# Attention and routed experts on one core: row maxima read from PSUM, low parts moved to GpSimd

## The chip, the cores and the metric

The kernel runs on one core of a Trainium2 chip. Five engines work at the same time, each through its own list of instructions in a fixed order: TensorE (PE in the profile, its weight loads PEld), VectorE (DVE), ScalarE (ACT), GpSimd (POOL) and SyncE (SP, which here issues most transfers). An instruction that waits holds up all that stand behind it on its engine. TensorE writes its results to PSUM, and VectorE and ScalarE read them there. The metric is the device time of one execution in microseconds.

## The reference

Two stages. Attention works on 2 batches x 8 heads, 768 tokens, 64 values a head; each query and key is assigned to the nearest of 16 centroids, and a query sees only keys of its own cluster:

```python
q_assign = argmax(q_n @ c_n)            # 16 centroids a head, all normalised
k_assign = argmax(k_n @ c_n)
mask = q_assign[:, :, :, None] == k_assign[:, :, None, :]
scores = where(mask, scale * q @ k.T, -1e9)
scores = scores - max(scores, axis=-1)
attn = exp(scores); attn = attn / (sum(attn) + 1e-9)
x = attn @ v                            # heads side by side: (2, 768, 512)
```

Then each token goes to one of 8 experts, chosen by the largest logit or, where a local gate says so, by the token before it; the output is the expert's probability times `relu(x @ w1[e]) @ w2[e]` (512 to 1024 to 512).

## The kernel before, in words

The sixteen heads are worked on in eight pairs `u`. 32-bit numbers go through TensorE as two 16-bit parts: a high part (a rounded copy) and a low part (the scaled value less the high part). For a pair, `stA` makes these parts of k, q and v. ScalarE makes the high parts (L216, L219, L226) and the 32-bit copy of v (`VF`, L228), VectorE the low parts in one instruction each (`lo`, L208), and VectorE copies the high parts of k and q into two more tiles, `K2` and `QM`, whose further columns take the cluster one-hots of `stB`, so that a product of `QM` and `K2` is a masked score. These two copies (L214) are called masked copies here. SyncE turns the tiles round by transposing transfers (K1T, QXT, K2T, QMT).

`stC` finds the row maxima. A head has nine units, each 256 queries by 256 keys: two matmuls (L320) into a PSUM tile `pm`, of which there are two in turn. In six of the nine units ScalarE copies `pm` to a 16-bit tile `ev` (L323), and VectorE later passes over each row of `ev` once (`tree`, L332); in the other three VectorE reduces `pm` itself (L325). `fin` then joins the maxima and writes them into `Q2` (L338 to L341), which SyncE transposes into `Q2T` (L342).

`stD` makes the attention of a head, again in nine units: four matmuls (L361, L362) that need K1T, Q1T, K2T and Q2T, an exponential on ScalarE (L364), and, five units later, the product with v. For units in `PVF` (four a head; all nine in the last head) this takes the 32-bit exponentials and `VF` (L389). For the others GpSimd subtracts the high part (`lo`, L370), and three 16-bit matmuls take the place of each 32-bit one (L391 to L393). `nm1` divides (L402 to L409), `nm2` on GpSimd makes the low part of the result `xt` (L413), which SyncE transposes and writes out (L489 to L492) for the logits.

`stC` runs 16 units ahead of `stD`. A hand-written list of places (`at`) gives every other step its place between units, and a scheduler then fixes the order of each engine's instructions when the kernel is built. The expert stage, after the last head, takes expert by expert: gather, two products, scatter; weights arrive in 512 KB pieces that ScalarE and VectorE split (L862, L864). A first expert is started while attention ends.

Of the kernel before, what the change touches and what calls it, by code (L numbers as in the profile page):

```python
# [7 lines left out]
F16 = mybir.dt.float16  # L8
# [14 lines left out]
KP = 28  # L23
# [11 lines left out]
WAX = 1  # L35
PVF = (1, 3, 5, 7)
NEQ = 2
NEM = 99
UORD = [(0, 0), (0, 1), (2, 0), (0, 2), (1, 0), (2, 1), (1, 1), (1, 2), (2, 2)]
OFFS = ((4, 0), (9, 1), (9, 2), (9, 3), (9, 4))  # L40
EVB = 2
EB = 7
K2E = 'V'
V0 = 1
# [5 lines left out]
NM2 = 'G'  # L50
SPLIT = ('kh', 'qh', 'vh', 'vf', 'kl', 'ql', 'vl')
TRO = 0
# [7 lines left out]
VP = -7.0  # L60
QME = 'V'
CAP_LEAD = (200, 176)
# [4 lines left out]
def tile_kernel(ctx, tc, q, k, v, centroids, w_gate, w_local, w1, w2, out):  # L67
# [131 lines left out]
    def stA(u, part=None):  # L199
        R = rows(part)  # L200
        hs = slice(0, 2) if part is None else slice(part, part + 1)

        def src(i):
            return f3(ld[u][i])[:, R]
        k1, k2, qx, qm, q2, vh, vl = (f3(rg(x, u))[:, R] for x in (K1, K2, QX, QM, Q2, VH, VL))

        def lo(out, x, h, sc):
            V.scalar_tensor_tensor(out=out, in0=x, scalar=sc, in1=h, op0=ALU.mult, op1=ALU.subtract)  # L208

        def cp(eng, out, x, h):  # L210
            if eng == "A":
                A.activation(out=out, in_=x, func=AF.Copy, scale=QS)
            else:
                V.tensor_copy(out, h)  # L214
        return dict(
            kh=lambda: A.activation(out=k1[:, :, 0:D], in_=src(0), func=AF.Copy, scale=QS),  # L216
            kl=lambda: lo(k1[:, :, D:2 * D], src(0), k1[:, :, 0:D], QS),
            kt=lambda: SP.dma_start_transpose(out=rg(K1T, u)[:, R], in_=flat(rg(K1, u)[:, hs])),
            qh=lambda: A.activation(out=qx[:, :, 0:D], in_=src(1), func=AF.Copy, scale=QS),  # L219
            ql=lambda: lo(qx[:, :, D:2 * D], src(1), qx[:, :, 0:D], QS),  # L220
            qt=lambda: SP.dma_start_transpose(out=rg(QXT, u)[:, R], in_=flat(rg(QX, u)[:, hs])),
            k2=lambda: cp(K2E, k2[:, :, 0:D], src(0), k1[:, :, 0:D]),
            qm=lambda: cp(QME, qm[:, :, 0:D], src(1), qx[:, :, 0:D]),
            q2=lambda: V.tensor_copy(q2[:, :, 0:D], qx[:, :, D:2 * D]),
            q1=lambda: [SP.dma_start(out=rg(Q1T, u)[i * D:i * D + D, R], in_=rg(QXT, u)[0:D, R]) for i in range(2)],
            vh=lambda: A.activation(out=vh[:, :, 0:D], in_=src(2), func=AF.Copy, scale=VS),  # L226
            vl=lambda: lo(vl, src(2), vh[:, :, 0:D], VS),
            vf=lambda: A.activation(out=f3(rg(VF, u))[:, R, 0:D], in_=src(2), func=AF.Copy, scale=VS),  # L228
        )

    def stB(u, part=None):
# [70 lines left out]
    def stC(g):  # L302
        u, hh = divmod(g, 2)
        st = {}
        order = UORD
        NEV = NEQ + (g % NEM == NEM - 1)
        NQ = 2 * NEV

        def unit(n):
            qp, kc = order[n]  # L310

            def f():
                if n == 0:
                    st["m"] = smp.tile([128, T], F32, name="m", tag="m", bufs=3)
                    st["mx"] = smp.tile([128, T, 3], F32, name="mx3", tag="mx3", bufs=3)
                    st["ev"] = smp.tile([128, 2 * NEV, 768], BF16, name="ev", tag="ev", bufs=EVB)
                pool, tag = (ps_s, "pst") if g == 0 and n % 2 else (ps_m, TM)
                ps = pool.tile([128, 2, 256], F32, name="pm", tag=tag)
                for i in range(2):
                    PE.matmul(out=ps[:, i], lhsT=rg(QMT, u)[:, hh * T + 2 * qp + i, :],  # L320
                              rhs=rg(K2T, u)[:, hh * T + 2 * kc:hh * T + 2 * kc + 2, :], start=True, stop=True)
                if qp < NEV:
                    A.activation(out=st["ev"][:, 2 * qp:2 * qp + 2, kc * 256:kc * 256 + 256], in_=ps, func=AF.Copy)  # L323
                else:
                    mark["V"] = V.tensor_reduce(out=st["mx"][:, 2 * qp:2 * qp + 2, kc], in_=ps, axis=AX.X, op=ALU.max).ins  # L325
            return f

        def tree(i):
            e = st["ev"]
            for j in ((0, 1), (2, 3), (4, 5), ())[i]:  # L330
                if j < 2 * NEV:
                    mark["V"] = V.tensor_scalar(out=e[:, j], in0=e[:, j], scalar1=1.0, scalar2=None, op0=ALU.mult, op1=ALU.max, accum_out=st["m"][:, j:j + 1]).ins  # L332
# [10 lines left out]
        return [unit(n) for n in range(9)], [lambda i=i: tree(i) for i in range(4)] if NQ else [], fin  # L343

    xt = {}

    def stD(g):
# [634 lines left out]
    if True:  # L982
# [44 lines left out]
        for u in range(NP):  # L1027
            a, bb = stA(u), stB(u)
            for nm in SPLIT:
                h2 = [stA(u, p)[nm] for p in range(2)]  # L1030
                a[nm] = lambda h2=h2: [f() for f in h2]
            c0 = 18 * u - LEAD
            if u == 0:
                at(c0 - 60, head0)
            else:
# [84 lines left out]
        for n in range(-90, last):  # L1120
# [6 lines left out]
            if 0 <= n < 9 * NH:  # L1127
# [3 lines left out]
                ds_[g][0][i]()  # L1131
            for off, what in OFFS:
                m = c - (off if c > 10 else min(off, 8))
                if 0 <= m < 9 * NH and m % 9 == 0:
                    if what < 4:
                        if cs_[m // 9][1]:
                            cs_[m // 9][1][what]()
                    else:
                        ins = cs_.pop(m // 9)[2]().ins
                        if m == 0:  # L1140
                            first[2] = ins
            m = n - PVL
# [121 lines left out]
```

## Time and profile before

| what | value |
|---|---|
| median of three runs | 469.55 us (463.31 to 472.13) |
| the profiled execution | 467.98 us, span 466.2 us |
| PE busy | 398.6 us (85%), PEld 349.1 us (75%) |
| DVE busy | 328.5 us (70%), 840 instructions |
| ACT busy | 269.7 us (58%), 508 instructions |
| POOL busy | 143.2 us (31%), 158 instructions |
| attention, the first to the last division of a head (L402) | starts at 57.7 and 270.9 us |
| mean granted clock of TensorE | 0.951 of 2.4 GHz |

Busy time says how much of the span an engine had work in hand, over stages with different limits; the stretch from 45 to 262 us holds most of attention and no expert but the first one's weights. A row of a group of instructions gives the line, engine, operation, tiles written and read, the shape, the count, then the total busy time and the mean of one in ns, then the idle time before them and what ended it. A row of a timeline gives the start and the length in us.

### The profile page before, as it was taken

How to read it: one execution, taken by the hardware profiler on the slowest of the kernel's cores; microseconds unless marked ns; L12 is line 12 of the kernel's file. 1: busy time of each engine (PE TensorE's matmuls, PEld its weight loads, DVE VectorE, ACT ScalarE, POOL GpSimd, SP SyncE). 2: the span in 40 equal slices, each digit the busy share in tenths (PEclk: the TensorE clock that was granted, in tenths of full speed). 3: DMA queues.
4: the chain of work that ended last, by engine and by line, in shares of the span. 5: the costliest groups of instructions: out<-in, count | busy, mean ns of one | idle time of the engine just before them, and what ended most of it. 6: DMA issues, size and time to landing. Idle time of an engine off the chain costs nothing. (4 is left out here: it accounts for less than half of the span.)

```text
span 466.2 us, 12705 instructions
## 1 busy us (share of the span) xinstructions
PE 398.6 (85%) x5039; PEld 349.1 (75%) x5039; DVE 328.5 (70%) x840; ACT 269.7 (58%) x508; POOL 143.2 (31%) x158
## 2 busy tenths in 40 slices
PE   0259879999888799989989999699998699999991
PEld 0237768888777789878879996697797497997870
DVE  7678985887969779787879158566683667666630
ACT  4268857686676767666886430235562656566430
POOL 3003434354343444434735301513022122201021
PEclk9998987999989999989999999799999799999996
DMA  8889998977936758247760712989698599796501
GB/s 171 137 180 206 287 186 194 206 160 155 187 86 139 140 91 159 53 86 161 182 193 19 142 35 55 289 255 231 172 339 305 169 316 277 255 300 215 190 30 33
DMA packets 125213, 81.45 MB, mean 175 GB/s; under 512 B 94537, under 2 KB 110153, under 8 KB 125152
## 3 DMA queue, kind: packets, MB, share of 16 engines
q1 hardware_dynamic: 122448, 73.47, 66.4%
q0 software_dynamic: 2704, 7.15, 4.9%
q8 instruction: 40, 0.66, 0.6%
q14 instruction: 21, 0.17, 0.1%
HBM read 47.04 MB, written 8.63 MB: 119 GB/s over the span
## 5 line engine op out<-in xcount | busy, mean ns | idle before, releaser
L370 POOL TENSOR_TENSOR lo<-e 128x512 f16<-128x512 f32 x75 | 82.2, 1100 | 135.5 <-ACT e L364 135.3
L864 DVE SCALAR_TENSOR_TENSOR W<-wst,W 128x1024 f16<-128x1024 f32 x64 | 77.9, 1222 | 31.6 <-ACT W L862 30.9
L364 ACT ACTIVATE e<-pst 128x512 f32<-128x512 f32 x144 | 83.3, 598 | 20.9 <-PE pst L362 18.9
L918 PE MATMUL g<-XT,W 128*128 128x200 f16 (+8 forms) x288 | 71.9, 261 | 10.0 <-DVE H L922 6.1
L362 PE MATMUL pst<-Q2T,K2T 128*128 128x256 f16 x288 | 74.4, 286 | 5.0 <-DMA Q2T<-Q 5.0
L361 PE MATMUL pst<-Q1T,K1T 128*128 128x256 f16 x288 | 75.1, 284 | 0.0
L389 PE MATMUL o<-VF,e 128*128 128x65 f32 x552 | 74.1, 273 | 0.0
L320 PE MATMUL pm<-K2T,QMT 128*128 128x256 f16 x288 | 55.4, 287 | 21.2 <-DVE mx L325 13.7
L862 ACT ACTIVATE W<-wst 128x1024 f16<-128x1024 f32 x64 | 66.7, 1051 | 9.9 <-DMA wst<-in_moe_w_dram 9.8
L919 PE MATMUL g<-XT,W 128*128 128x200 f16 (+8 forms) x288 | 71.9, 261 | 0.0
L389 PEld LDWEIGHTS o<-VF,e 128*128 128x128 f32 x552 | 70.7, 197 | 1.1
L920 PE MATMUL g<-XT,W 128*128 128x200 f16 (+8 forms) x288 | 70.1, 261 | 0.0
L323 ACT ACTIVATE ev<-pm 128x512 bf16<-128x512 f32 x96 | 55.7, 594 | 20.2 <-PE pm L320 19.9
L332 DVE TENSOR_SCALAR_CACHE_REDUCE ev<-ev 128x768 bf16<-128x768 bf16 x64 | 58.2, 945 | 7.9 <-ACT ev L323 7.9
L921 ACT ACTIVATE H<-g 128x200 f16<-128x200 f32 (+8 forms) x72 | 24.3, 343 | 63.4 <-PE g L920 53.9
L320 PEld LDWEIGHTS <-QMT 128*128 128x128 f16 x288 | 25.3, 106 | 27.7 <-issue 20.5
L391 PE MATMUL o<-VH,e 128*128 128x65 f16 x300 | 40.3, 197 | 0.0
L922 DVE SCALAR_TENSOR_TENSOR H<-g,H 128x200 f16<-128x200 f32 (+8 forms) x72 | 25.9, 373 | 20.2 <-ACT H L921 16.1
L392 PE MATMUL o<-VL,e 128*128 128x64 f16 x300 | 40.1, 195 | 0.0
L929 POOL DMA_INDIRECT out_dram<-ob,scim x16 | 17.7, 1105 | 72.7 <-ACT ob L927 37.6
L393 PE MATMUL o<-VH,lo 128*128 128x65 f16 x300 | 39.4, 196 | 0.0
L361 PEld LDWEIGHTS <-K1T 128*128 128x128 f16 x288 | 31.1, 108 | 9.4 <-issue 5.7
(301 smaller groups left out, 929.2 us busy)
## 6 DMA issues: line engine op xcount, KB each, us to landing
wst<-in_moe_w_dram SPq DMA_DIRECT2D x64, 512.0 KB
xd<-xt SPq DMA_DIRECT2D x12, 384.0 KB
ld_k<-in_k_dram SPq DMA_DIRECT2D x7, 384.0 KB
ld_q<-in_q_dram SPq DMA_DIRECT2D x7, 384.0 KB
ld_v<-in_v_dram SPq DMA_DIRECT2D x7, 384.0 KB
Q1T<-QXT SPq DMA_DIRECT2D x14, 192.0 KB
ld_k<-in_k_dram SPq DMA_DIRECT2D x2, 192.0 KB
ld_q<-in_q_dram SPq DMA_DIRECT2D x2, 192.0 KB
```

The costliest lines, as they stand in the source:

```text
L320: PE.matmul(out=ps[:, i], lhsT=rg(QMT, u)[:, hh * T + 2 * qp + i, :], rhs=rg(K2T, u)[:, hh * T + 2 * kc:hh * T + 2 * kc + 2, :], start=Tru ...
L332: mark["V"] = V.tensor_scalar(out=e[:, j], in0=e[:, j], scalar1=1.0, scalar2=None, op0=ALU.mult, op1=ALU.max, accum_out=st["m"][:, j:j + 1 ...
L361: PE.matmul(out=ps[:, i], lhsT=rg(K1T, u)[:, j, :], rhs=rg(Q1T, u)[:, hh * T + 2 * qc:hh * T + 2 * qc + 2, :], start=True, stop=False)
L362: PE.matmul(out=ps[:, i], lhsT=rg(K2T, u)[:, j, :], rhs=rg(Q2T, g)[:, 2 * qc:2 * qc + 2, :], start=False, stop=True)
L364: mark["A"] = A.activation(out=e, in_=ps.rearrange("p a b -> p (a b)"), func=AF.Exp, scale=SCL).ins
L370: G.tensor_tensor(out=lo, in0=e, in1=eh, op=ALU.subtract)
L389: PE.matmul(out=o[:, t, 0:65], lhsT=e[:, sl], rhs=vf[:, hh, j, 0:65], start=first, stop=False, skip_group_check=True)
L862: A.activation(out=h[:, cs], in_=s[:, cs], func=AF.Copy, scale=WS)
L864: V.scalar_tensor_tensor(out=l[:, cs], in0=s[:, cs], scalar=WS, in1=h[:, cs], op0=ALU.mult, op1=ALU.subtract)
L918: PE.matmul(out=ps, lhsT=lh, rhs=XT[:, 2 * kk, 0:cap], start=(kk == 0), stop=False)
L919: PE.matmul(out=ps, lhsT=lh, rhs=XT[:, 2 * kk + 1, 0:cap], start=False, stop=False)
L920: PE.matmul(out=ps, lhsT=ll, rhs=XT[:, 2 * kk, 0:cap], start=False, stop=(kk == KD - 1))
```

## The change

From the third pair on (`u > 1`) ScalarE scales k and q in place, GpSimd makes all low parts by a plain subtraction, and the high parts are copies of the scaled values; v's low part is taken from `VF`. The masked copies go to ScalarE, and so do two small operations of `vs2`. All nine units of a head are reduced by VectorE from PSUM; `ev`, `tree` and the ScalarE copies are gone, and `fin` has one place in the order. `PVF` has three units in place of four.

```diff
-PVF = (1, 3, 5, 7)
-OFFS = ((4, 0), (9, 1), (9, 2), (9, 3), (9, 4))
-K2E = 'V'
-QME = 'V'
+PVF = (1, 4, 7)
+FINO = 9
+K2E = 'A'
+QME = 'A'
...
+        def scaled(i):
+            if u > 1:
+                A.activation(out=src(i), in_=src(i), func=AF.Copy, scale=QS)
+        def hi(out, i):
+            A.activation(out=out, in_=src(i), func=AF.Copy, scale=1.0 if u > 1 else QS)
         def lo(out, x, h, sc):
-            V.scalar_tensor_tensor(out=out, in0=x, scalar=sc, in1=h, op0=ALU.mult, op1=ALU.subtract)
+            if u > 1:
+                G.tensor_tensor(out=out, in0=x, in1=h, op=ALU.subtract)
+            else:
+                V.scalar_tensor_tensor(out=out, in0=x, scalar=sc, in1=h, op0=ALU.mult, op1=ALU.subtract)
...
-            V.tensor_scalar(out=tf[96:98], in0=st["vs"][96:98], scalar1=1.0 / S, scalar2=None, op0=ALU.mult)
-            V.tensor_copy(tm[96:98], tf[96:98])
+            A.activation(out=tf[96:98], in_=st["vs"][96:98], func=AF.Copy, scale=1.0 / S)
+            A.activation(out=tm[96:98], in_=tf[96:98], func=AF.Copy)
...
-                if qp < NEV:
-                    A.activation(out=st["ev"][:, 2 * qp:2 * qp + 2, kc * 256:kc * 256 + 256], in_=ps, func=AF.Copy)
-                else:
-                    mark["V"] = V.tensor_reduce(out=st["mx"][:, 2 * qp:2 * qp + 2, kc], in_=ps, axis=AX.X, op=ALU.max).ins
+                mark["V"] = V.tensor_reduce(out=st["mx"][:, 2 * qp:2 * qp + 2, kc], in_=ps, axis=AX.X, op=ALU.max).ins
-        def tree(i):
...
-            if NEV < 3:
-                V.tensor_reduce(out=m[:, 2 * NEV:T], in_=st["mx"][:, 2 * NEV:T], axis=AX.X, op=ALU.max)
+            V.tensor_reduce(out=m, in_=st["mx"], axis=AX.X, op=ALU.max)
...
-                    lo = ep.tile([128, 512], F16, name="lo", tag="lo", bufs=5)
+                    lo = ep.tile([128, 512], F16, name="lo", tag="lo", bufs=6)
...
-                    for i, nm in enumerate(("kh", "kl", "kt", "qh", "ql", "qt")):
-                        at(max(c0 - KP + 1.5 * i, L2P + 0.1 * i + 0.1), a[nm])
+                    for i, nm in enumerate(("k", "q")):
+                        for p in range(2):
+                            for j, w in enumerate("shl"):
+                                x = 4.5 * i + 1.5 * p + 0.5 * j
+                                at(max(c0 - KP + x, L2P + 0.1 * x + 0.1), hv[nm + w][p])
```

What the change makes of the order shows at three places. First VectorE, after the small tile `DV` of one pair is written, in the kernel before (`pm` is a score buffer, `mx` its maxima, `ev` the 16-bit copy, K and QX the tiles with low parts):

```order
L287 SCALAR_TENSOR_TENSOR DV_122<-tm,w_104,tf 2x2x64
L325 TENSOR_REDUCE mx_1941<-pm 128x2
L214 COPY K_107<-K_106 128x12x64
L332 TENSOR_SCALAR ev,m<-ev 128x768 x2
L208 SCALAR_TENSOR_TENSOR K_106<-ld_k,K_106 128x6x64 x2
L325 TENSOR_REDUCE mx_1941<-pm 128x2
L214 COPY QM_109<-QX_108 128x12x64
L505 TENSOR_TENSOR acc_537<-lg,acc_537 128x108
L332 TENSOR_SCALAR ev,m<-ev 128x768 x2
L325 TENSOR_REDUCE mx_1941<-pm 128x2
```

The same place in the changed kernel:

```order
L297 SCALAR_TENSOR_TENSOR DV_122<-tm,w_104,tf 2x2x64
L328 TENSOR_REDUCE mx_1969<-pm 128x2 x2
L398 TENSOR_SCALAR r<-o 128x6
L399 RECIPROCAL r<-r 128x6
L401 TENSOR_TENSOR xf<-o,r 128x384
L328 TENSOR_REDUCE mx_1969<-pm 128x2 x5
L501 TENSOR_TENSOR acc_531<-lg,acc_531 128x108
L334 TENSOR_REDUCE m<-mx_1969 128x6
```

Between the reductions there stood two passes over `ev` and the low parts; now there stand reductions and the small operations of `nm1` and `fin`.

GpSimd, in the middle of attention, had `lo` blocks with one `xt` of each head between them and nothing else. In the changed kernel it has, there:

```order
L214 TENSOR_TENSOR VL_117<-VF_120,VH_114 128x384
L409 TENSOR_TENSOR xt<-xf,xt 128x6x64
L366 TENSOR_TENSOR lo<-e 128x512 x4
L214 TENSOR_TENSOR QX_108<-ld_q,QX_108 128x6x64 x2
L214 TENSOR_TENSOR K_106<-ld_k,K_106 128x6x64
L214 TENSOR_TENSOR VL_117<-VF_120,VH_114 128x384
L214 TENSOR_TENSOR K_106<-ld_k,K_106 128x6x64
L366 TENSOR_TENSOR lo<-e 128x512 x2
L409 TENSOR_TENSOR xt<-xf,xt 128x6x64
```

Six low parts a pair stand among the `lo` blocks now, up to five of them in a row, ahead of the `lo` and `xt` behind them.

SyncE, at the end of the first head of a pair, in the kernel before:

```order
L342 DMA_TRANSPOSE Q2T_139<-Q_111 128x6x128
L489 DMA_TRANSPOSE xT<-xt 128x12x128
L490 DMA xd<-xt 768x1x256
L492 DMA xd_61<-xt 768x1x256
L221 DMA_TRANSPOSE QXT_128<-QX_108 128x12x128
L342 DMA_TRANSPOSE Q2T_140<-Q_110 128x6x128
```

and in the changed kernel:

```order
L185 DMA ld_v<-in_v_dram 128x2x384
L231 DMA_TRANSPOSE QXT_128<-QX_108 128x12x128
L485 DMA_TRANSPOSE xT<-xt 128x12x128
L486 DMA xd<-xt 768x1x256
L488 DMA xd_61<-xt 768x1x256
L338 DMA_TRANSPOSE Q2T_140<-Q_110 128x6x128
```

QXT, which reads a low part of q, has moved ahead of the transfers of `xt`; Q2T stands last in both.

## Rows read from the trace of the kernel before

**Rows 1.** Stretches: busy us of PE, PEld, DVE, ACT, POOL; clock, DMA share, GB/s.

```profile
45.00:262.00 217.00, 196.91 (x2679) 177.39 (x2679) 174.93 (x416) 154.28 (x304) 94.68 (x88) 0.95 0.72 150
262.00:466.20 204.20, 182.10 (x2129) 156.66 (x2126) 118.24 (x297) 91.34 (x155) 41.49 (x39) 0.95 0.68 200
```

**Rows 2.** TensorE's waits from 45 to 262 us: total us, times, longest.

```profile
PE pm L320 <- DVE mx L325: 11.9, 13, 2.5
PE pst L362 <- DMA Q2T<-Q: 5.0, 6, 1.1
PE pm L320 <- ACT ev L323: 2.7, 4, 1.3
```

**Rows 3.** Busy times as in the first group, two stretches at the lower clock.

```profile
65.60:75.80 10.20, 9.27 (x66) 7.31 (x63) 5.18 (x12) 6.89 (x14) 2.90 (x3) 0.50 1.12 243
...
161.10:164.50 3.40, 3.25 (x25) 2.66 (x25) 2.19 (x7) 2.15 (x6) 1.04 (x1) 0.50 0.63 119
```

**Rows 4.** Timeline (start us, us) of VectorE, GpSimd and TensorE around one wait.

```profile
54.14 0.54 DVE L208 SCALAR_TENSOR_TENSOR K<-ld_k,K 128x384 f16<-128x384 f32 x1
...
126.59 2.35 POOL L370 TENSOR_TENSOR lo<-e 128x512 f16<-128x512 f32 x2 [1.81 <-ACT e L364]
126.66 2.69 DVE L208 SCALAR_TENSOR_TENSOR K<-ld_k,K 128x384 f16<-128x384 f32 x2
129.28 0.68 DVE L325 TENSOR_REDUCE mx<-pm 128x2 f32<-128x512 f32 x1
130.01 0.38 PE L320 MATMUL pm<-K2T,QMT 128*128 128x256 f16 x2 [2.07 <-DVE mx L325]
```

**Rows 5.** Groups of instructions by form, from 45 to 262 us.

```profile
L370 POOL TENSOR_TENSOR lo<-e 128x512 f16<-128x512 f32 x72 | 79.0, 1103 | 104.8 <-ACT e L364 104.7
L332 DVE TENSOR_SCALAR_CACHE_REDUCE ev<-ev 128x768 bf16<-128x768 bf16 x56 | 50.9, 945 | 7.9 <-ACT ev L323 7.9
L323 ACT ACTIVATE ev<-pm 128x512 bf16<-128x512 f32 x82 | 47.9, 593 | 14.3 <-PE pm L320 14.0
L325 DVE TENSOR_REDUCE mx<-pm 128x2 f32<-128x512 f32 x42 | 28.8, 686 | 5.1 <-PE pm L320 4.9
L413 POOL TENSOR_TENSOR xt<-xf,xt 128x384 f16<-128x384 f32 x14 | 13.9, 992 | 16.8 <-ACT xt L409 16.8
L208 DVE SCALAR_TENSOR_TENSOR QX<-ld_q,QX 128x384 f16<-128x384 f32 x12 | 10.5, 913 | 0.1
L208 DVE SCALAR_TENSOR_TENSOR VL<-ld_v,VH 128x384 f16<-128x384 f32 x12 | 9.3, 780 | 0.1
L208 DVE SCALAR_TENSOR_TENSOR K<-ld_k,K 128x384 f16<-128x384 f32 x10 | 8.7, 886 | 0.6 <-ACT K L216 0.6
```

**Rows 6.** TensorE's timeline: a 32-bit block, a 16-bit block, and what follows each.

```profile
157.21 1.00 PE L389 MATMUL o<-VF,e 128*128 128x65 f32 x8
158.05 0.30 PE L499 MATMUL lg<-wg,xT 128*128 128x18 f16 x6
...
167.15 0.19 PE L391 MATMUL o<-VH,e 128*128 128x65 f16 x1
...
167.51 0.28 PE L361 MATMUL pst<-Q1T,K1T 128*128 128x256 f16 x1
```

**Rows 7.** Groups of ScalarE by form, whole span.

```profile
L228 ACT ACTIVATE VF<-ld_v 128x384 f32<-128x384 f32 x14 | 7.2, 529 | 1.1 <-PE o L389 0.6 <-DMA ld_v<-in_v_dram 0.3
...
L226 ACT ACTIVATE VH<-ld_v 128x768 f16<-128x768 f32 x1 | 0.8, 834 | 0.0
```

**Rows 8.** TensorE's timeline: three more of its waits for VectorE.

```profile
65.05 0.38 PE L320 MATMUL pm<-K2T,QMT 128*128 128x256 f16 x2 [1.61 <-DVE mx L325]
...
145.07 0.38 PE L320 MATMUL pm<-K2T,QMT 128*128 128x256 f16 x2 [1.86 <-DVE mx L325]
...
161.25 0.58 PE L320 MATMUL pm<-K2T,QMT 128*128 128x256 f16 x2 [2.52 <-DVE mx L325]
```

**Rows 9.** SyncE's waits from 45 to 262 us: total us, times, longest.

```profile
SPq L489 <- POOL lo L370: 15.5, 5, 8.7
```

More of the change, by code (lines that the diff above doesn't have):

```diff
@@ L50 @@
 NM2 = 'G'
-SPLIT = ('kh', 'qh', 'vh', 'vf', 'kl', 'ql', 'vl')
+SPLIT = ('ks', 'kh', 'qs', 'qh', 'vh', 'vf', 'kl', 'ql', 'vl')
 TRO = 0
@@ L205, in stA @@
         k1, k2, qx, qm, q2, vh, vl = (f3(rg(x, u))[:, R] for x in (K1, K2, QX, QM, Q2, VH, VL))
+        def scaled(i):
[3 more added lines that the diff above has]
+            A.activation(out=out, in_=src(i), func=AF.Copy, scale=1.0 if u > 1 else QS)
         def lo(out, x, h, sc):
-            V.scalar_tensor_tensor(out=out, in0=x, scalar=sc, in1=h, op0=ALU.mult, op1=ALU.subtract)
+            if u > 1:
+                G.tensor_tensor(out=out, in0=x, in1=h, op=ALU.subtract)
+            else:
+                V.scalar_tensor_tensor(out=out, in0=x, scalar=sc, in1=h, op0=ALU.mult, op1=ALU.subtract)
         def cp(eng, out, x, h):
             if eng == "A":
-                A.activation(out=out, in_=x, func=AF.Copy, scale=QS)
+                A.activation(out=out, in_=x, func=AF.Copy, scale=1.0 if u > 1 else QS)
             else:
@@ L215, in stA @@
         return dict(
-            kh=lambda: A.activation(out=k1[:, :, 0:D], in_=src(0), func=AF.Copy, scale=QS),
+            ks=lambda: scaled(0),
+            kh=lambda: hi(k1[:, :, 0:D], 0),
             kl=lambda: lo(k1[:, :, D:2 * D], src(0), k1[:, :, 0:D], QS),
             kt=lambda: SP.dma_start_transpose(out=rg(K1T, u)[:, R], in_=flat(rg(K1, u)[:, hs])),
-            qh=lambda: A.activation(out=qx[:, :, 0:D], in_=src(1), func=AF.Copy, scale=QS),
+            qs=lambda: scaled(1),
+            qh=lambda: hi(qx[:, :, 0:D], 1),
             ql=lambda: lo(qx[:, :, D:2 * D], src(1), qx[:, :, 0:D], QS),
@@ L226, in stA @@
             vh=lambda: A.activation(out=vh[:, :, 0:D], in_=src(2), func=AF.Copy, scale=VS),
-            vl=lambda: lo(vl, src(2), vh[:, :, 0:D], VS),
+            vl=lambda: lo(vl, f3(rg(VF, u))[:, R, 0:D] if u > 1 else src(2), vh[:, :, 0:D], VS),
             vf=lambda: A.activation(out=f3(rg(VF, u))[:, R, 0:D], in_=src(2), func=AF.Copy, scale=VS),
@@ L304, in stC @@
         st = {}
-        order = UORD
-        NEV = NEQ + (g % NEM == NEM - 1)
-        NQ = 2 * NEV
         def unit(n):
-            qp, kc = order[n]
+            qp, kc = UORD[n]
             def f():
@@ L342, in fin @@
             return SP.dma_start_transpose(out=rg(Q2T, g), in_=q2.rearrange("p t d -> p (t d)"))
-        return [unit(n) for n in range(9)], [lambda i=i: tree(i) for i in range(4)] if NQ else [], fin
+        return [unit(n) for n in range(9)], fin
     xt = {}
@@ L1028, in tile_kernel @@
             a, bb = stA(u), stB(u)
+            hv = {nm: [stA(u, p)[nm] for p in range(2)] for nm in SPLIT}
             for nm in SPLIT:
-                h2 = [stA(u, p)[nm] for p in range(2)]
-                a[nm] = lambda h2=h2: [f() for f in h2]
+                a[nm] = lambda h2=hv[nm]: [f() for f in h2]
             c0 = 18 * u - LEAD
@@ L1054, in tile_kernel @@
                         at(L2P, load2)
-                    for i, nm in enumerate(("kh", "kl", "kt", "qh", "ql", "qt")):
-                        at(max(c0 - KP + 1.5 * i, L2P + 0.1 * i + 0.1), a[nm])
+                    for i, nm in enumerate(("k", "q")):
[3 more added lines that the diff above has]
+                                at(max(c0 - KP + x, L2P + 0.1 * x + 0.1), hv[nm + w][p])
+                        x = 4.5 * i + 3.5
+                        at(max(c0 - KP + x, L2P + 0.1 * x + 0.1), a[nm + "t"])
                     for i in range(4):
@@ L1069, in tile_kernel @@
                     at(c0 - 3, a["q1"])
-                    at(c0 - 16.2, a["vh"])
-                    at(c0 - 15, a["vl"])
-                    at(c0 - 14.5, a["vf"])
+                    for p in range(2):
+                        at(c0 - 16.2 + 2 * p, hv["vf"][p])
+                        at(c0 - 15.7 + 2 * p, hv["vh"][p])
+                        at(c0 - 15.2 + 2 * p, hv["vl"][p])
                     at(c0 - 7.5, bb["vs"])
@@ L1131, in tile_kernel @@
                 ds_[g][0][i]()
[L1132 to L1141, printed above, removed]
+            m = c - (FINO if c > 10 else 8)
+            if 0 <= m < 9 * NH and m % 9 == 0:
+                ins = cs_.pop(m // 9)[1]().ins
+                if m == 0:
+                    first[2] = ins
             m = n - PVL
```

8 lines of the change are left out of this document (removed).

## The prediction

> **What bounds the kernel now.** I read the busy times by stretch first, then TensorE's waits in the attention stretch, then the granted clock behind those waits, then single timelines around a wait.
>
> The attention stretch, 45 to 262 us, is nearly half of the span [rows 1]. TensorE is busy in 196.91 of its 217.00 us, VectorE in 174.93, ScalarE in 154.28, GpSimd in 94.68. So TensorE sets the pace, VectorE is the next engine at 81%, and GpSimd has more than half its time free. The reader is to see that 20.1 us of TensorE's stretch are idle, and that three waits account for nearly all of them [rows 2]: 11.9 us for a score buffer (`pm`) that VectorE has not yet read, 5.0 us for the transposed Q2T, 2.7 us for a `pm` that ScalarE has not yet copied out. The granted clock is the second loss. In four pieces of the stretch, of 10.2, 3.4, 3.4 and 3.4 us, it is 0.50, the lower level of 1.2 GHz [rows 3], where the first and the third of them stand; each follows one or two waits of TensorE of 0.9 to 2.5 us. Work at half the clock loses at most half of the 20.4 us, 10.2 us.
>
> What makes VectorE late is in [rows 4]. TensorE waits 2.07 us for a `pm`, until 130.01. In that time VectorE runs two low-part instructions on L208, 2.69 us for the two, while GpSimd runs two `lo` subtractions, 2.35 us for the two; only then does VectorE start the reduction at 129.28 that frees the buffer. The same form on L208 takes 0.54 us at 54.14, where GpSimd is not shown with it. The mean of the form in the stretch is 0.78 to 0.91 us [rows 5], so this collision is common and not a single event.
>
> **The change part by part**, in the profiled execution of 467.98 us, which is 1.6 us under the median of the three runs.
>
> Three 32-bit blocks a head instead of four. A 32-bit block takes TensorE from 157.21 to 158.05, 0.84 us; a block of twelve 16-bit matmuls from 167.15 to 167.51, 0.36 us [rows 6]. Fifteen heads change one block (the last head stays all 32-bit): 15 x 0.48 = 7.2 us of TensorE's own time at the full clock. Nothing lies beside it, because TensorE is the pacing engine. **-7.2 us**, bounds 0 (were each saving eaten by a wait) and 7.2.
>
> Row maxima straight from PSUM. The stretch holds 82 ScalarE copies, 47.9 us, and 56 passes over the copied rows on VectorE, 50.9 us [rows 5]. They give way to 82 more reductions of 0.686 us, 56.3 us. On VectorE alone the swap costs 5.4 us. TensorE's wait for ScalarE's copy can't occur any more: **-2.7 us**. But all nine units of a head now wait for VectorE, where three did. The Trainium skill (VectorE: DVE Perf Modes, Rules for kernel authors) speaks against this edit: a reduction is the slowest VectorE operation, to be restructured on a hot path, and a matmul's output may rather be copied to SBUF first. By that rule VectorE gets longer, which the 56.3 against 50.9 bears out; taken alone it would add up to 5.4 us where I book a gain.
>
> Low parts of q, k, v to GpSimd. From the third pair on, 36 instructions leave VectorE. The stretch has 34 on L208, 28.5 us, of which the four of the second pair stay (about 3.4), so some 25 us go [rows 5]. VectorE's balance is 174.9 - 50.9 - 25 + 56.3, at most 155 us, and less by the masked copies and the small operations on `tf` and `tm`, which leave too. GpSimd gets 36 x 0.992 (the form 128x384 of L413) = 35.7 us and 15 x 1.103 = 16.5 us for the fifteen new `lo` blocks: 94.7 becomes 146.9 us, 74% of a stretch of 198 us. ScalarE loses 47.9 and gets 24 in-place scalings x 0.529 = 12.7 us, 14 wide masked copies x 0.834 = 11.7 us [rows 5, 7] and some twenty smaller ones, below 0.53 us each: still under 145 us. The exponentials that TensorE needs sit behind these on ScalarE; I cost that at nothing because ScalarE's idle share grows. If that cover is gone, an exponential starts one copy, 0.83 us, late.
>
> VectorE's wait, now 11.9 us over 13 times. Four waits make 8.06 us of it: 2.07 [rows 4], 1.61, 1.86 and 2.52 [rows 8]. By VectorE's timeline ahead of each, the three of 2.07, 1.86 and 2.52 us, 6.45 together, stand behind L208 or the passes on L332, which leave; the one of 1.61 stands behind L208 and behind a one-hot product and a small line of `fin` that stay. One end is 0. The other end goes with the number of units: the remaining 5.45 us over the 48 units that VectorE reads are 0.114 us a unit, and 144 units would make 16.3 us, more than now. I take 6, nearer to the lower end, since much of the 5.45 us stood behind leaving work too: **-5.9 us**, bounds -11.9 and +4.4.
>
> Clock. Three of the four slow pieces, 3.4 us each, follow waits for VectorE or ScalarE of 1.3 to 2.5 us. If those waits shrink the pieces go: half of 10.2 is **-5.1 us**. The first piece, 65.6 to 75.8, I leave: it has a Q2T wait in it and the DMA share of its stretch is 1.12 [rows 3]. Bounds 0 and 10.2.
>
> What is late next. SyncE issues the transposes in order. The one of `xt` already waits 15.5 us for GpSimd [rows 9], and the Q2T of the odd head stands behind it (the last place shown in the part on the change). With the low parts in front of it on GpSimd, `xt` comes up to three instructions of 0.99 us later, and so do K1T and QXT, which now wait for GpSimd themselves. TensorE's 5.0 us for Q2T therefore stay, and I add **+3.0 us**, one such delay; bounds 0 and one delay in each of the eight pairs, 24 us, of which the free time on SyncE hides most.
>
> Sum: 467.98 - 7.2 - 2.7 - 5.9 - 5.1 + 3.0 = 450.1. The stretches before 45 and after 262 us keep their work; the start's reductions on VectorE (9 x 0.686 = 6.2 us a head) take the place of copies and passes that took it about as long. I predict **450 us** for the median.
>
> **Rivals.**
> - *All of it goes.* VectorE is never late, the clock stays up, Q2T comes in time: 467.98 - 7.2 - 11.9 - 2.7 - 5.0 - 10.2 = 431. For it: the waits' cause leaves. Against: Q2T's chain gets GpSimd ahead of it. 431 to 440 has a chance of 0.13.
> - *The waits only change their names.* The block swap and ScalarE's wait are gained, the rest comes back as short waits: 468 - 9.9 = 458, and up to 463. For it: VectorE stays above 70% and collides more often with a GpSimd that is busy 74% instead of 44% of the stretch, in the instructions that it keeps (one-hot products, the q copy, the DV line). 0.19, two thirds of it below 460.2. The Trainium skill (GPSIMD Engine Reference, 8. Key points) has the rule for it: GpSimd shares its SBUF interfaces with VectorE and contends with VectorE instructions that have two SBUF inputs; the trace agrees (1.35 us each in rows 4, 0.54 alone).
> - *VectorE's wait goes with the units* (slower). If each unit that VectorE reads costs what it does now, 11.9/48 = 0.25 us, then 144 units cost 35.7: 468 + 23.8 - 9.9 = 482. It decides from 21.8 us of such waits, 0.15 us a unit. Against it: 6.45 of the 11.9 us stand behind instructions that leave. 0.05.
> - *GpSimd becomes the bound* (slower). Its 139 instructions in the stretch at a mean of 1.63 us would take 226 us: 477. It decides from a mean of 1.42 us (198 us); now it is 94.68/88 = 1.08, and 1.17 in the collision of rows 4. 0.04. The Trainium skill (GPSIMD Engine Reference, 4.1 Engine selection) says not to put two-input elementwise work on GpSimd, being about twice as slow; the trace agrees (0.99 against 0.54), and this is the rule by which the move would lose.
> - *No effect*: the stretch is not on the path, and what follows waits for something else. TensorE is busy 182.10 of the 204.20 us after it [rows 1], so an earlier end moves everything. 468, 0.06.
>
> **How the numbers follow.** The forecast, 442 to 457, has 0.53. This kernel's runs spread from 463.3 to 472.1, so 2%, 9.4 us, is about what can be told; the line is 460.2. Faster: 0.53 + 0.13 + 0.12 = 0.78. Same: 0.07 + 0.06 = 0.13. Slower: 0.09. The range 437 to 462 leaves out the lower half of the first rival, the slower cases and no effect, about 0.21.
>
> **What would show it.** In the changed profile: 360 matmuls on each of the three 16-bit lines and 432 on the 32-bit one; the mean of the reductions still near 0.69 us; TensorE's `pm` waits at about 6 us for VectorE and none for ScalarE; VectorE's busy time in attention under 155 us, GpSimd's near 147 with a mean near 1.05; fewer pieces at 0.50. The prediction is wrong if `pm` waits stay above 12 us, if Q2T waits grow past 8 us, or if TensorE waits for GpSimd's `lo` or `VL`.

## The result, and the profile after

The changed kernel takes 449.19 us (median of four executions) where the kernel before took 467.87 us beside it on the same chip: a ratio of 0.962, with a 95% interval of 0.951 to 0.973. One of the four took 969.08 us at a granted clock of 1.0, for a reason that no trace shows; the ratio leaves it out, as it does the longest of the kernel before, 472.13 us, and the other three, 447.58 to 449.77 us, have a median of 448.62. The forecast was 450. The profiled execution has 447.58 us and a span of 445.8 us, at a mean granted clock of 0.979 instead of 0.951.

The stretches after, with the columns of [rows 1], and below them the only piece of attention that is left at the lower clock [rows 3]:

```profile
45.00:241.60 196.60, 179.10 (x2686) 161.91 (x2682) 143.51 (x322) 130.28 (x259) 135.98 (x135) 0.99 0.76 155
241.60:445.80 204.20, 182.06 (x2155) 157.24 (x2153) 119.37 (x300) 93.00 (x157) 42.50 (x40) 0.96 0.70 205
48.20:51.60 3.40, 3.06 (x36) 2.22 (x37) 1.25 (x2) 3.04 (x7) 2.62 (x4) 0.50 1.04 289
```

The second row is cut to the length of the second stretch of before, 204.20 us counted back from the end, and holds the same work (TensorE busy 182.06 us, before 182.10): the gain lies ahead of it, as the prediction had it. VectorE fell from 81% to 73% of the attention stretch, GpSimd rose from 44% to 69%. TensorE's waits in attention, to be held against [rows 2]:

```profile
PE pst L357 <- ACT e L360: 5.3, 9, 1.2
PE pm L326 <- DMA QMT<-QM: 4.9, 3, 2.3
PE pm L326 <- DVE mx L328: 2.6, 8, 0.7
PE sim L259 <- DMA K1T<-K: 2.6, 1, 2.6
PE rp L533 <- DVE sc L531: 1.5, 1, 1.5
```

All three waits of before are gone or small: VectorE 11.9 to 2.6 us, ScalarE's copy 2.7 to none, Q2T 5.0 to none. But 14.3 us of new ones (5.3 + 4.9 + 2.6 + 1.5) stand in their place, so TensorE is idle for 17.5 of 196.6 us where it was for 20.1 of 217. The groups that answer to [rows 5]:

```profile
L366 POOL TENSOR_TENSOR lo<-e 128x512 f16<-128x512 f32 x86 | 92.8, 1094 | 43.2 <-ACT e L360 43.1
L328 DVE TENSOR_REDUCE mx<-pm 128x2 f32<-128x512 f32 x123 | 82.1, 685 | 28.2 <-PE pm L326 28.0
L409 POOL TENSOR_TENSOR xt<-xf,xt 128x384 f16<-128x384 f32 x14 | 13.5, 966 | 4.5 <-ACT xt L405 4.5
L214 POOL TENSOR_TENSOR QX<-ld_q,QX 128x384 f16<-128x384 f32 x12 | 10.8, 923 | 3.6 <-DVE r L398 1.5 <-DVE Q L234 1.4 <-ACT QX L210 0.8
```

The reduction costs 685 ns as before (686), the low part on GpSimd 923, and `lo` stayed at 1,094 (1,103) although GpSimd has much more to do. GpSimd still waits 43 us for exponentials, so it isn't the bound.

Where the new waits come from is seen on ScalarE and TensorE around one of them (start us, us):

```profile
98.69 0.94 ACT L210 ACTIVATE K<-ld_k 128x384 f16<-128x384 f32 x2 [2.53 <-DMA K1T<-K]
99.53 0.58 ACT L360 ACTIVATE e<-pst 128x512 f32<-128x512 f32 x1
100.16 0.27 PE L357 MATMUL pst<-Q1T,K1T 128*128 128x256 f16 x1 [1.22 <-ACT e L360]
```

ScalarE stands 2.53 us before a copy of the next pair, because the tile of the high and low parts of k (`K1` in the kernel, `K` in the row) has one buffer and the transposition of the pair before still reads it. The exponential behind it in ScalarE's list comes late, and TensorE waits 1.22 us for it. The masked copies that moved to ScalarE wait in the same way, for the tile `K2`, which the row calls `K` too:

```profile
ACT K L220 <- DMA K2T<-K: 8.1, 5, 3.6
```

### The profile page after: what moved, and what is told of

Its sections match the earlier page's. It is cut to its first block, busy times and chain, and to the rows that moved or that the text cites. A ratio compares the mean times of both kernels' runs of the same rounds, so it can differ in the third digit from the quotient of the medians.

```text
span 445.8 us, 12748 instructions
## 1 busy us (share of the span) xinstructions
PE 384.8 (86%) x5099; PEld 336.4 (75%) x5099; DVE 296.4 (66%) x738; ACT 248.6 (56%) x470; POOL 189.5 (43%) x209
## 5 line engine op out<-in xcount | busy, mean ns | idle before, releaser
L366 POOL TENSOR_TENSOR lo<-e 128x512 f16<-128x512 f32 x90 | 96.9, 1091 | 72.5 <-ACT e L360 72.4
L328 DVE TENSOR_REDUCE mx<-pm 128x2 f32<-128x512 f32 x144 | 95.7, 685 | 30.7 <-PE pm L326 30.4
L358 PE MATMUL pst<-Q2T,K2T 128*128 128x256 f16 x288 | 71.1, 273 | 0.0
L385 PE MATMUL o<-VF,e 128*128 128x65 f32 x432 | 56.7, 270 | 0.0
L385 PEld LDWEIGHTS o<-VF,e 128*128 128x128 f32 x432 | 53.4, 192 | 0.7
L388 PE MATMUL o<-VL,e 128*128 128x64 f16 x360 | 47.1, 192 | 0.0
L387 PE MATMUL o<-VH,e 128*128 128x65 f16 x360 | 47.0, 194 | 0.0
L389 PE MATMUL o<-VH,lo 128*128 128x65 f16 x360 | 44.0, 193 | 0.4 <-POOL lo L366 0.4
L901 POOL DMA_INDIRECT xg<-xd,gim x16 | 16.8, 1049 | 50.5 <-DMA XT<-xg 38.6
L915 PEld LDWEIGHTS <-W 128*128 128x128 f16 x288 | 28.6, 99 | 9.6 <-issue 7.2
```

Source lines behind the costliest of these rows:

```text
L358: PE.matmul(out=ps[:, i], lhsT=rg(K2T, u)[:, j, :], rhs=rg(Q2T, g)[:, 2 * qc:2 * qc + 2, :], start=False, stop=True)
L385: PE.matmul(out=o[:, t, 0:65], lhsT=e[:, sl], rhs=vf[:, hh, j, 0:65], start=first, stop=False, skip_group_check=True)
L915: PE.matmul(out=ps, lhsT=lh, rhs=XT[:, 2 * kk + 1, 0:cap], start=False, stop=False)
```

## The experiments

For every run I read the same ledger from its profiled execution, in attention from 45 us to the last head's division: TensorE's idle time in waits, the part of it for VectorE's maxima and for Q2T, and what the clock cost (half of the time at 0.50, an upper bound). The last column is read off TensorE's order: how many units of scores stand between a head's last unit of maxima and its own first unit of scores, the mean over heads 3 to 16. `fin` and the transposition Q2T have to fit in there; it is called the lead below.

| run | median us | ratio to before (95%) | last division | idle | VectorE | Q2T | clock | lead |
|---|---|---|---|---|---|---|---|---|
| before | 465 to 468 | | 270.9 | 19.9 | 11.9 | 5.0 | 10.2 | 5.4 |
| changed | 449.19 | 0.962 (0.951 to 0.973) | 252.2 | 16.9 | 2.6 | 0 | 1.7 | 6.9 |
| e1 four blocks | 453.78 | 0.973 (0.967 to 0.978) | 257.4 | 12.9 | 3.0 | 0.4 | 6.8 | 7.5 |
| e2 three blocks alone | 469.22 | 1.004 (1.000 to 1.009) | 269.7 | 26.3 | 9.0 | 8.2 | 8.5 | 4.3 |
| e3 PSUM maxima alone | 454.09 | 0.972 (0.966 to 0.978) | 257.7 | 10.4 | 5.0 | 2.5 | 1.7 | 5.2 |
| e4 low parts alone | 476.14 | 1.023 (1.016 to 1.029) | 277.7 | 25.5 | 4.7 | 13.3 | 6.8 | 2.6 |
| e5 PSUM maxima, three blocks | 454.23 | 0.974 (0.968 to 0.979) | 258.6 | 14.5 | 10.0 | 3.0 | 5.1 | 4.6 |
| e6 as e4, masked copies on VectorE | 476.53 | 1.025 (1.018 to 1.031) | 278.8 | 27.4 | 4.3 | 15.9 | 8.5 | 2.6 |
| e7 changed, two buffers | 447.59 | 0.958 (0.952 to 0.964) | 252.0 | 13.2 | 4.0 | 0.7 | 5.1 | 7.2 |
| e8 changed, masked copies on VectorE | 450.53 | 0.966 (0.961 to 0.971) | 255.6 | 13.2 | 6.5 | 0 | 8.5 | 7.1 |
| e11 changed, low parts on VectorE | 455.94 | 0.978 (0.974 to 0.983) | 254.6 | 18.4 | 6.3 | 5.3 | 1.7 | 5.3 |
| e12 changed, two buffers and two blocks | 467.10 | none (458.26 to 469.50) | 271.3 | 28.8 | 6.7 | 4.7 | 13.7 | 7.9 |

e9 and e10 are told apart below. One row is one execution, and not always one near the median: that of e2, 461.61 us, is the shortest of twelve, that of e11, 451.08, the shortest of six, that of e3, 456.49, the longest of six. With 448.62 in place of 449.19 for the changed kernel each difference from it below is 0.6 us larger; with only three executions behind it, its interval overlaps those of e1 and e5, so differences of 5 us are best estimates.

**e1: the change with four 32-bit blocks a head.**

```diff
-PVF = (1, 4, 7)
+PVF = (1, 3, 5, 7)
```

> The changed kernel with four 32-bit blocks a head again, all else as changed. Theory (TensorE paces attention with its own work): each of 15 blocks costs 0.48 us more, so 449 + 7.2 = 456 us, TensorE's waits from 45 us to the end of attention stay near 17 us. Rival (the block swap is swallowed by waits for GpSimd and ScalarE, whose fifteen lo blocks leave here): within 2 us of 449.

453.78 against 449.19: within the full change the swap is worth 4.6 us of the 7.2. TensorE waits in e1:

```profile
PE pst L357 <- ACT e L360: 4.9, 5, 3.0
PE pm L326 <- DVE mx L328: 3.0, 7, 0.9
```

In attention TensorE is busy 9.3 us longer than in the changed kernel (199.0 against 189.7), of which up to 5.1 belong to the clock (6.8 against 1.7), and idle 4.0 us less. So the swap's work is partly taken back in the changed kernel as waits, the one for QMT above all (4.9 against 1.8 here). Neither forecast is met: the time lies between the two, and the waits fell to 12.9 us.

**e2: three blocks alone, on the kernel before.**

```diff
-PVF = (1, 3, 5, 7)
+PVF = (1, 4, 7)
```

> The kernel before with three 32-bit blocks a head, nothing else changed. Theory: TensorE has 7.2 us less work but VectorE's collisions with GpSimd stay and get fifteen lo instructions more, so less than the full 7.2 us arrives: 462 to 466 against 468. Rival (the swap is worth the same anywhere): 460.5.

469.22, no gain in the median (1.004, 1.000 to 1.009); both forecasts had one. The twelve executions spread from 461.61 to 474.41 us, and even the three shortest, with a mean of 464.0, are only 2.4 us below the mean of the kernel before, a third of the 7.2. TensorE's waits:

```profile
PE pm L320 <- DVE mx L325: 9.0, 9, 1.7
PE pst L362 <- DMA Q2T<-Q: 8.2, 5, 3.1
```

TensorE has the shorter work, and waits instead: its idle time is 26.3 instead of 19.9 us.

**e3: maxima from PSUM alone, on the kernel before** (with the one place of `fin`; low parts, copies and blocks as before).

```diff
-                if qp < NEV:
-                    A.activation(out=st["ev"][...], in_=ps, func=AF.Copy)
-                else:
-                    mark["V"] = V.tensor_reduce(...)
+                mark["V"] = V.tensor_reduce(...)
```

> The kernel before with all row maxima read from PSUM by VectorE, nothing else changed (four blocks, low parts and masked copies still on VectorE). Theory (the relief of VectorE comes from the low parts, the maxima alone lengthen it by about 5 us): TensorE waits more than 11.9 us for VectorE and none for ScalarE; 466 to 474. Rival (the two-step way through ScalarE and back was the late part): waits for VectorE under 6 us, 455 to 460.

454.09, 12.2 us below the kernel before: this part alone brings two thirds of the whole. My theory fails, and what the rival said of the waits holds, at a time just below its range. The edit takes out ScalarE's copies and VectorE's passes together; which of the two is worth the 12.2 us no run separates. Its stretch:

```profile
45.00:248.00 203.00, 191.46 (x2709) 174.36 (x2708) 170.79 (x389) 116.57 (x222) 97.00 (x90) 0.99 0.78 159
```

TensorE's waits in it:

```profile
PE pm L316 <- DVE mx L318: 5.0, 14, 0.5
PE pst L348 <- DMA Q2T<-Q: 2.5, 3, 1.3
```

VectorE is fuller than before (84% of the stretch, before 81%) and yet less late: the longest wait for it is 0.5 us instead of 2.5. The stretch is at clock 0.99.

**e4: the low parts alone, on the kernel before** (scaling in place, plain subtraction on GpSimd, masked copies and two small operations of `vs2` on ScalarE, all at the places that they have in the changed kernel's order).

```diff
-K2E = 'V'
+K2E = 'A'
-QME = 'V'
+QME = 'A'
...
+            if u > 1:
+                G.tensor_tensor(out=out, in0=x, in1=h, op=ALU.subtract)
```

> The changed kernel with the row maxima as before (ScalarE copies, passes on VectorE) and four 32-bit blocks, so that only the low parts on GpSimd, the in-place scaling and the masked copies on ScalarE are left of the change (lo has five buffers as before, for space). Theory (collisions of low parts with GpSimd made VectorE late): TensorE's waits for VectorE fall from 11.9 to under 5 us, 456 to 460. Rival (VectorE's passes over the copies made it late, or ScalarE, at 154 + 25 us of work, becomes late): waits for a pm of 10 us or more, 464 to 470.

476.14, slower by 1.6 to 2.9%, which neither forecast had. Two lines of TensorE and one of VectorE show how:

```profile
PE pst L375 <- DMA Q2T<-Q: 13.3, 10, 3.4
PE pm L333 <- DVE mx L338: 4.7, 8, 0.9
...
DVE ev L345 <- ACT ev L336: 23.1, 13, 5.0
```

The wait that the low parts were blamed for falls from 11.9 to 4.7 us, as the prediction wanted, but the wait for Q2T grows by 8.3. VectorE now stands 23.1 us (before 7.9 [rows 5]) for ScalarE's 16-bit copies, with the masked copies, the scalings and the exponentials on ScalarE as well; and the lead in TensorE's order fell to 2.6 units.

**e5: maxima from PSUM and three blocks.**

```diff
-PVF = (1, 3, 5, 7)
+PVF = (1, 4, 7)
```

(on e3)

> The kernel before with the row maxima read from PSUM and three 32-bit blocks a head; low parts and masked copies stay on VectorE. Theory now (reading PSUM directly is what ends VectorE's lateness, the low parts' move gives nothing of its own): the block swap brings its 4.6 us on top of 454.1, so 448 to 451, as the whole change. Rival (with fifteen more lo blocks the low parts on VectorE collide with GpSimd, as where the block swap alone brought nothing): 454 to 458, and the move of the low parts is worth the difference to 449.

454.23, as e3 and as the rival had it. The swap's gain goes into one wait:

```profile
PE pm L316 <- DVE mx L318: 10.0, 14, 1.8
PE pst L348 <- DMA Q2T<-Q: 3.0, 4, 0.9
```

GpSimd has fifteen more `lo` blocks, and VectorE is busy in 178.59 of the 204 us from 45 us on. During these 14 waits and the 1.5 us ahead of each, VectorE spends 10.2 us on low parts and masked copies; in e3 it spent 3.5 there.

**e6: e4 with the masked copies back on VectorE.**

```diff
-K2E = 'A'
+K2E = 'V'
-QME = 'A'
+QME = 'V'
```

> The version with only the low parts moved (row maxima through ScalarE copies, four blocks, 476 us), with the masked copies of k and q back on VectorE. Theory (ScalarE, which got scalings and masked copies and waits in order for transposes, makes its copies of pm late, these VectorE's passes, these the maxima and Q2T): VectorE's wait for those copies falls from 23.1 us to under 12, TensorE's wait for Q2T from 13.3 to under 8, 466 to 470. Rival (the low parts on GpSimd hold up the transposes on SyncE): Q2T waits stay above 11 us, 474 to 478.

476.53, with 15.9 us for Q2T in 12 waits. That the masked copies on ScalarE made e4 slow is refuted; VectorE's wait for ScalarE's copies fell only to 19.5 us. The rival's numbers came true, but not its reason. VectorE, SyncE and TensorE around the longest of the 12 waits (start us, us):

```profile
82.74 0.16 DVE L354 TENSOR_SCALAR Q<-m 128x12 f16<-128x12 f32 x1
82.93 1.21 SPq L355 DMA_TRANSPOSE Q2T<-Q  x1
87.29 0.37 PE L375 MATMUL pst<-Q2T,K2T 128*128 128x256 f16 x1 [3.23 <-DMA Q2T<-Q]
```

SyncE starts the transposition 0.03 us after the last write of `fin`, and within 0.13 us in all 12, so no low part holds it up there; in e4 it does so in eight of the ten and is 1.4 and 1.5 us late in two. It is `fin` that comes late for TensorE's order. What e4 and e6 share, and no other run has, is the lead of 2.6 units, with the low parts on GpSimd beside maxima that go through `ev`.

**e7: the changed kernel with two buffers for `K2` and `QM`.**

```diff
-    K2 = ring(tokp, "K2", [128, 2, T, 128], F16, 1)
+    K2 = ring(tokp, "K2", [128, 2, T, 128], F16, 2)
-    QM = ring(tokp, "QM", [128, 2, T, 128], F16, 1)
+    QM = ring(tokp, "QM", [128, 2, T, 128], F16, 2)
```

> The changed kernel with two buffers instead of one for the masked tiles K2 and QM, all else as changed. Theory (ScalarE waits up to 3.6 us in its order for the transposes of these tiles, 9.7 us in all, and the exponentials and QMT behind it come late): these waits go, TensorE's waits for exponentials and QMT (10.2 us) halve, 442 to 446. Rival (the waits are slack of ScalarE, the transposes are late for SyncE's own order): 448 to 451.

```profile
PE pm L326 <- DVE mx L328: 4.0, 11, 0.7
...
PE pst L357 <- ACT e L360: 1.6, 4, 0.8
PE pm L326 <- DMA QMT<-QM: 1.0, 1, 1.0
```

The waits named fall as the theory has it, from 5.3 to 1.6 us for exponentials and from 4.9 to 1.0 for QMT. The time is 447.59, between the two forecasts, and its interval overlaps that of the changed kernel: of the 7.6 us won, 3.9 came back as other waits, and up to 3.4 went to the clock (5.1 us instead of 1.7). It is the fastest kernel here by its median, but it isn't shown to be faster than the change. `K1`, whose wait was shown above as the example, kept its one buffer, and ScalarE still waits for it (4.9 us in the change):

```profile
ACT K L210 <- DMA K1T<-K: 6.0, 2, 3.8
```

So, by this run, most of the late exponentials came from the masked tiles and not from `K1`.

**e8: the changed kernel with the masked copies on VectorE.**

```diff
-K2E = 'A'
+K2E = 'V'
-QME = 'A'
+QME = 'V'
```

> The changed kernel with the masked copies of k and q back on VectorE (K2E and QME), all else as changed. Theory (in-order waits on ScalarE delay exponentials): waits of TensorE for exponentials fall from 5.3 us to under 2, waits for VectorE rise from 2.6 us by less than 3: 446 to 450. Rival (VectorE, now in front of every pm, must not wait for transposes): waits for VectorE above 7 us, 452 to 456.

450.53: the place of the masked copies is worth 1 or 2 us, if anything; the intervals overlap. VectorE's wait grows to 6.5 us, by more than the theory allowed and less than the rival wanted; the one for exponentials falls to 2.5.

**e9: the kernel before with more lead, e10: with more lead and three blocks.**

```diff
-LEAD = 16
+LEAD = 20
```

(e10 also with `PVF = (1, 4, 7)`)

> The kernel before with the maxima 20 instead of 16 units ahead of attention; no work is removed. Theory (the first half of attention before is bound by a chain of each head: last maxima, their joining, the transpose Q2T, first score): the Q2T waits of 5.0 us fall below 2 and part of the 11.9 us for VectorE with them, so the time is 458 to 463 us. Rival (VectorE's own amount of work makes the waits): more lead only moves them, Q2T falls but the waits for VectorE stay at 10 us or more, 464 to 469 us.

> The kernel before with 20 units of lead and three 32-bit blocks a head. Theory (three blocks bring their 7.2 us wherever the chain of Q2T has slack): 4 to 7 us below the run with 20 units of lead and four blocks. Rival (the fifteen more 16-bit blocks bring fifteen more subtractions on GpSimd, which lengthen VectorE's low parts and copies, so VectorE takes the gain): within 1.5 us of that run, with waits for VectorE of 9 us or more.

In both the parts of v of a later pair are written, with a lead of 20, into a tile that the last products of an earlier head still have to read (in e9 those of the fourth pair from 56.87 us on, while the second head's last product starts at 71.0), so x is another one and the experts get other tokens. The whole times, 499.22 and 493.50 us (1.071 and 1.057), are therefore not comparable, and only attention is read. In e9 the wait for Q2T falls to 2.0 us, and nothing is won: the last division starts at 279.7, later than before's 270.9, and the waits for VectorE stay:

```profile
PE pm L320 <- DVE mx L325: 10.3, 12, 1.9
...
PE pst L362 <- DMA Q2T<-Q: 2.0, 3, 1.4
```

The theory that the chain through Q2T alone bounds the kernel before falls; the rival's wait is there, though both missed the time. In e10 the order keeps a lead of only 4.8 units and the wait for Q2T is back at 9.8 us. Attention is 7.3 us shorter than in e9 (272.4 against 279.7), near the 7.2 of the swap, and the whole 5.7 us, as the theory had it, although the chain of Q2T has no slack there and VectorE's low parts are where they were. So the swap can pay without the other parts; but e10's attention is still longer than before's, and no version that is faster than before shows this.

**e11: the changed kernel with its low parts on VectorE**, same instruction, other engine.

```diff
-                G.tensor_tensor(out=out, in0=x, in1=h, op=ALU.subtract)
+                V.tensor_tensor(out=out, in0=x, in1=h, op=ALU.subtract)
```

> The changed kernel with the low parts from the third pair on back on VectorE, as the same plain subtraction of in-place scaled values; all else as changed. Theory (with three blocks VectorE is the engine that lacks room, and the move to GpSimd makes it): VectorE goes from 70% to about 82% of attention, waits for VectorE from 2.6 to 7 to 10 us, time 453 to 457 us. Rival (the room on VectorE is not needed, masked copies on ScalarE made it already): 447 to 451 us.

455.94, 6.8 us above the change and as slow as e5, as the theory has it. VectorE's share of the time from 45 us to the last division is 79%, by the same count 70% in the change, and the wait for it is 6.3 us, a little less than forecast; and the lead is down to 5.3 units, with Q2T back:

```profile
PE pm L326 <- DVE mx L328: 6.3, 10, 1.5
PE pst L358 <- DMA Q2T<-Q: 5.3, 5, 3.2
```

**e12: two 32-bit blocks a head, on e7.**

```diff
-PVF = (1, 4, 7)
+PVF = (2, 6)
```

> The changed kernel with two buffers for K2 and QM, and two instead of three 32-bit blocks a head. Theory (TensorE sets the pace, so that each block swapped gives its 0.48 us fifteen times): 7.2 us below the run with two buffers alone (447.6), less up to half of it in new waits, 440 to 444 us. Rival (GpSimd, at 66% of attention, gets fifteen more subtractions of 1.09 us and is late with lo and the low parts): 446 to 452 us, with waits of TensorE for lo, K1T or QXT of over 6 us together.

467.10, with runs from 458.26 to 469.50, so spread that no ratio is given; each of them is slower than any run of e7. Both theories missed it, and the first fails outright: less work for TensorE doesn't go on paying. The waits that the rival named, for `lo`, K1T and QXT, come to 2.5 us instead of over 6. The longer ones, in an execution of 467.77 us (what the one of 458.26 waited for isn't known):

```profile
PE pst L357 <- ACT e L360: 7.7, 5, 2.5
PE pm L326 <- DVE mx L328: 6.7, 13, 1.2
...
ACT e L360 <- PE o L388: 17.8, 21, 5.2
```

ScalarE waits 17.8 us (1.0 in the change) for a product that still reads the buffer of an exponential, and TensorE in turn for exponentials. The lead swings from 7 to 12 units and ends at 3 and 1 in the last two heads. Whether the order or GpSimd's `lo` makes these products late I didn't test.

## Why the prediction was right

The total is right, 450 against 449.19, and so is the place; several of its steps were not, and their errors cancel, so that a microsecond separates the two is luck. In the two profiled executions attention ends 18.7 us earlier (270.9 to 252.2), of 20.4 us in the span. Of the 18.7, TensorE's busy time gives 16.1 (205.8 to 189.7) and its waits 3.0 (19.9 to 16.9), less 0.4 that rounding and small gaps leave. The sum had the swap and the clock at 12.3 and the waits at 5.6. The signs that it named are there: no wait for ScalarE's copy, VectorE busy 143.5 us (forecast under 155), GpSimd 136.0 (near 147).

- *The block swap, -7.2, "nothing lies beside it, because TensorE is the pacing engine"*: the work is gone (16.1 us of busy time less 8.5 of clock leave 7.6), but that it is worth 7.2 is wrong as a rule. It was worth 4.6 in the full change (e1), nothing that can be told on the kernel before (e2) and nothing on PSUM maxima alone (e5), where VectorE's wait grew by 5.0. The lower bound, each saving eaten by a wait, is what two of these three cases come near to. TensorE set the pace only between its waits.
- *ScalarE's copy, -2.7*: right, no such wait is left in the change and in e3.
- *VectorE's wait, -5.9*: 9.3 went. The direction is right, the cause half. The 13 waits of before have, in them and in the 1.5 us ahead of each, 9.1 us of low parts and masked copies on VectorE and 9.0 us of passes over `ev`. Taking either away leaves less than half: 5.0 us without the passes (e3), 4.7 without the low parts and masked copies (e4). I had put the low parts first [rows 4] and booked the maxima as 5.4 us more on VectorE. The rule of the Trainium skill that I weighed there (VectorE: DVE Perf Modes, Rules for kernel authors) would have made this edit a loss; VectorE got fuller in e3, as it says, and the kernel 12.2 us faster, so the measurement decides against it. The page advises the copy to SBUF only for many operations on the output, which I didn't say there; here each copied row got one pass.
- *Clock, -5.1*: 8.5 went (10.2 to 1.7). The first piece, which I left, went as well. The loss doesn't follow the sum of the waits: e3 has 1.7 at 10.4 us idle, the change 1.7 at 16.9, e7 and e8 5.1 and 8.5 at 13.2. Single microseconds of it are not to be forecast from this.
- *Q2T stays at 5.0 and +3.0 is added*: wrong, it went to none. This is the step that failed. I looked at what stands ahead of the transposition on SyncE [rows 9]; but in four of the six waits of before SyncE started it within 0.1 us of the last write of `fin`, so it wasn't SyncE that made those. In the change SyncE does wait for the low parts as foreseen:

```profile
SPq L231 <- POOL VL L214: 12.0, 4, 4.6
```

  It costs nothing: the new order has 6.9 units between a head's last maxima and its first scores instead of 5.4. The transposition that SyncE starts latest, at 125.17, 2.95 us after `fin`, isn't needed until 133.77. Over all runs the wait for Q2T goes with that number: 13.3 and 15.9 us at 2.6 units, 3.0 to 9.8 at 4.3 to 4.8, 2.5 to 5.3 at 5.2 to 5.4, and at most 0.7 from 6.9 on (but for e9 with 2.0, and e12 with its uneven 4.7). In e9, where the lead alone was raised (5.4 to 7.1), the wait fell from 5.0 to 2.0; elsewhere the engines changed with it. That lead is a property of the built order, which a reader could count before running anything; the prediction shows SyncE's order and didn't count TensorE's.
- *Left out of the sum*: 14.3 us of new waits for exponentials, QMT, K1T and one small product. The prediction said of exponentials that they come late if ScalarE's cover is gone and costed it at nothing, because ScalarE's idle share grows. That share did grow (29% to 34% of the stretch), but part of it is now ScalarE standing ahead of an exponential before a copy into a single-buffered tile. e7 shows it for QMT and the masked copies.

The parts don't add up: alone they change the time by -12 (maxima), +10 (low parts) and +3 us (blocks, by the medians; the interval just reaches none), together -17 to -19. With the maxima from PSUM, the low parts' move is worth nothing at four blocks (e1 453.8, e3 454.1) and 5.0 at three (449.2, e5 454.2); the swap is worth nothing that can be told without the move (e2, e5) and 4.6 with it. e11 and e5, both with three blocks, PSUM maxima and the low parts on VectorE, differ in all else that came with the move (scaling in place, masked copies on ScalarE, places, a sixth `lo` buffer) and take 455.94 and 454.23 us: so it is the engine of the low parts that brings the 5.0. My reading is that the move makes the room on VectorE that the fifteen more `lo` blocks need; the order changes with it (a lead of 5.3 and 4.6 against 6.9), and no run parts the two. The rival "the waits only change their names" is partly what happened, with names that, K1T apart, stood on no list of mine.

What stays open: why the low parts alone leave the order only 2.6 units of lead. The order is made from the whole program when the kernel is built; I couldn't hold it fixed while an engine was changed.

## What to carry to other kernels

A saving on the busiest engine is not worth its time everywhere: here the same swap brought 4.6 us with the change's other parts and nothing that can be told without them (e2, e5), so measure it again after each wait that is removed. Where a scheduler orders the lists, count in the new order how far each result is made ahead of its use; here that number went with the Q2T wait, while VectorE's load, counted to the last division, went against it (60% in e4 with 13.3 us, 81% in e3 with 2.5). And when copies move to the engine that feeds TensorE, look for one that writes a single-buffered tile: all that stands behind it waits for that tile's last reader.

## What the runs showed of the hardware

VectorE's reductions aren't lengthened by GpSimd, several of its other operations are. In the kernel before, from 45 to 262 us, a reduction from PSUM takes 686 ns on average while GpSimd runs an elementwise operation (26 of them) and 685 without (16); a low part on VectorE takes 1,049 ns (21) against 550 (13). That it was read from PSUM isn't what spared the reduction: one within SBUF (L265) takes 549 ns beside GpSimd and 547 without (three each). Even a tiny operation can be held for the length of a GpSimd instruction. In the changed kernel, VectorE and GpSimd around one of them (start us, us):

```profile
164.43 0.18 DVE L336 TENSOR_SCALAR Q<-m 128x6 f16<-128x6 f32 x1
164.50 1.02 DVE L337 TENSOR_SCALAR Q<-m 128x12 f16<-128x12 f32 x1
...
164.44 2.05 POOL L366 TENSOR_TENSOR lo<-e 128x512 f16<-128x512 f32 x2 [1.71 <-ACT e L360]
```

The 128x12 operation starts just after a `lo` and ends about when the first `lo` of two does; at ten of its fourteen places in attention it takes 0.16 to 0.17 us, at the other four 0.42 to 1.02. Its mean before, where GpSimd had less to do and the hold fell on the line ahead of it instead (L340, up to 1.02 us):

```profile
L341 DVE TENSOR_SCALAR Q<-m 128x12 f16<-128x12 f32 x14 | 2.3, 166 | 0.0
```

and in the changed kernel:

```profile
L337 DVE TENSOR_SCALAR Q<-m 128x12 f16<-128x12 f32 x14 | 5.0, 356 | 0.0
```

The Trainium skill (SBUF — State Buffer, Who interferes with whom) has this as a lock, for VectorE instructions that use both ports for one input or have two inputs in SBUF: whichever of VectorE and GpSimd starts first holds the shared port pair for its whole instruction, and the other stands still. The trace agrees with the hold, with 1.02 us for an operation of 0.17; which ports this operation uses no run here shows. That reductions are spared doesn't explain why the move of row maxima was a gain: the passes over `ev` that they replaced were not held up themselves (none took over 954 ns, beside GpSimd or not); they only stood in the list, two or more in a row.
